# Moving a key norm, four weight scans and two weight loads in the first layer of a linear-attention kernel

## The chip, the cores and the metric

The kernel runs on one core of a Trainium2 chip. The metric is device time in microseconds (us) of one execution of the whole program. Executions of one kernel on one chip mostly agree within some 0.3%. The share of TensorE's full speed that the profile shows for a stretch is called the granted clock; 0.50 is "half clock". Chips differ a little. Kernels are compared only within the same rounds.

## The reference, cut to what matters

Two blocks, each run twice with the same weights: linear attention (A), then a gated bilinear block (B). S is 2048, D 1024, 32 heads of 32, F 3584, all weights in bf16.

```python
def _A_ref(x, wqkv, wo):
    q, k, v = ...                                  # x @ wqkv, in heads
    phi = lambda t: jnp.where(t > 0, t + 1, jnp.exp(t)) + 1e-6
    pq, pk = phi(q), phi(k)
    kv = jnp.einsum("bhsd,bhse->bhde", pk, v)
    z = jnp.einsum("bhsd->bhd", pk)
    num = jnp.einsum("bhqd,bhde->bhqe", pq, kv)
    den = jnp.einsum("bhqd,bhd->bhq", pq, z)[..., None] + 1e-6
    return (num / den)... @ wo

x = A_x
x = x + _A_ref(_layernorm(x), A_wqkv, A_wo)
x = x + _B_ref(_layernorm(x), B_w_gate, B_w_up, B_w_down)   # (g * u) @ w_down
# ... and both once more
```

The kernel works partly in f16, and scales its operands by norms of weights. So it needs, once, a sum of squares of the key weights (the "key norm") and of the three large matrices of block B (the "scans": 42 pieces of 512 KB, each loaded, squared and summed by one ScalarE instruction). All this happens in the first layer, beside its matmuls.

## The kernel before

The stages of the first layer, in TensorE's order: key projection ("k stage"); products of key features with the normalised input, mixed with query tiles ("x and q stage"); values times that ("kv"), query tiles mixed with small products with the output weights ("join"); the output tiles; then block B, the second layer. The parts that the change touches:

```python
def load_o():                                    # output weights, 2 x 1 MB, ScalarE's queue
    for n in range(2):
        nc.scalar.dma_start(out=wo[n], in_=wo_v[:, :, n * NB:(n + 1) * NB])

wv = [head(3), head(1)]                          # value weights live in K[3] and K[1] ...
scan_a = [K[i][:, j * 2 * D:(j + 1) * 2 * D] for i in (3, 1) for j in range(2)]   # ... where early scans do

EARLY, MID, SYNC = 24, 32, 16
scan_buf = [scan_a[i % 4] for i in range(EARLY)] + [scan_c[i % 4] for i in range(NSCAN - EARLY)]

def scan_fetch():                                # loads go out as far ahead as buffers allow
    while scanned[1] < scanned[2]:
        i = scanned[1]
        if any(scan_buf[j] is scan_buf[i] for j in range(scanned[0], i)) or i >= max(EARLY, scanned[0] + 3):
            return
        (nc.sync if i < SYNC else nc.gpsimd).dma_start(out=scan_buf[i], in_=scan_src(i))
        scanned[1] += 1

def scan_step(n=1):
    for _ in range(n):
        i = scanned[0]
        m, c = divmod(i, NU)
        nc.scalar.activation(out=scan_buf[i], in_=scan_buf[i], func=ACT.Square, accum_out=acc[:, m, c:c + 1])
        scanned[0] += 1
        if i in (EARLY - 3, EARLY - 1):          # a buffer is free: value weights, 1 MB each
            n = (i - EARLY + 3) // 2
            nc.scalar.dma_start(out=wv[n], in_=wqkv_v[:, :, 2 * D + n * NB:2 * D + (n + 1) * NB])
        scan_fetch()

# k stage, unit i of the loop (two units are one tile of 128 rows from tile 4 on)
if i == 2:      # sum of squares of each partition's key weights
    nc.vector.tensor_reduce(out=part[:, 3:4], in_=acc[:, 3:4, :], axis=AX.X, op=ALU.add)
elif i == 3:    # 4 bytes a partition to DRAM ...
    nc.sync.dma_start(out=WS[:, :], in_=part[:, 3:4])
elif i == 6:    # ... and back as a row to every partition
    nc.sync.dma_start(out=row, in_=WS[:, :].rearrange("p o -> o p").to_broadcast([P, P]))
elif i == 8:
    nc.vector.tensor_reduce(out=part[:, 3:4], in_=row, axis=AX.X, op=ALU.add)
    ...                                          # maximum, power -1/2
elif i == 9:
    scale_bits(3, 4)
    key_scale()

# end of the x and q stage
x_add(3, 1, QP[b1])
scanned[2] = MID
scan_fetch()
q(7, b0, 2)
scan_step(1)
q(8, a1, 1)
scan_step(1)
q(9, b1, 1)
scan_step(1)
q(10, b0, 2)
load_o()
scan_step(1)
```

## Time and profile before

| | before |
|---|---|
| time, median of 3 runs | 1491.86 us (1490.99 to 1492.01) |
| span of the profiled run | 1488.0 us |
| TensorE without a matmul | 19.0 us |
| k stage ends (first product of the next stage) | 73.92 us |
| kv starts | 164.52 us |
| first output tile starts | 197.60 us |
| first product with TX of block B starts | 256.33 us |

The last four are starts in TensorE's timeline. They cut the run into stretches that each have their own limit. The prediction shows the lines of the waits, of the k stage and of the join. In all such lines, K, ST, TX, XT, MX, W and Q are buffers of the program (Q is the PSUM banks that TensorE writes), and ACTq, SPq or POOL with a DMA is that engine issuing a transfer. Two more rows of the kernel before are needed later, from TensorE's timeline where block B begins (start, duration, then the instruction; a wait would stand in brackets):

```profile
252.88 3.62 PE L1008 MATMUL Q<-XT,K 128*128 128x512 bf16 x16
256.33 1.89 PE L1008 MATMUL Q<-TX,K 128*128 128x512 f16 x8
```

There is no wait between the two rows.

### The profile page before, as it was taken

The numbers are of one execution on the slowest core, as the hardware profiler recorded it, in microseconds if no ns is written. First come the engines' busy times: TensorE is split into PE (matmuls) and PEld (weight loads), VectorE is DVE, ScalarE is ACT, GpSimd is POOL, SyncE is SP. The second block draws the span as 40 slices with busy tenths as digits, with TensorE's granted clock in tenths as the row PEclk, the third lists the DMA queues.
The fourth block names the chain that finished last, engine by engine and source line by source line (L and its number), as shares of the span: only waits on it lengthen the run. The fifth ranks groups of instructions, "written<-read, shape, count | busy, mean of one in ns | idle before, by whom it ended". The sixth has DMA issues, their size and how long they took to land. (4 is left out here: it accounts for less than half of the span.)

```text
span 1488.0 us, 17649 instructions
## 1 busy us (share of the span) xinstructions
PE 1469.0 (99%) x6913; PEld 668.1 (45%) x6913; DVE 1056.5 (71%) x1577; ACT 744.5 (50%) x693; POOL 103.3 (7%) x230
## 2 busy tenths in 40 slices
PE   9899899999999999999999999999999999999999
PEld 3344444444444444444444445444444444444444
DVE  7676788988866477776479778867776845777532
ACT  6678687787700355550087347545563015566200
POOL 2201112000001000000042000200000100000000
PEclk9999999999999999999999999999999999999999
DMA  6466958697647333325739444353332753333442
GB/s 179 119 200 199 282 116 194 199 268 213 214 148 218 82 94 93 88 85 182 221 85 241 71 132 95 64 127 92 86 86 99 243 164 95 85 85 85 154 166 84
DMA packets 267443, 213.29 MB, mean 143 GB/s; under 512 B 102240, under 2 KB 250336, under 8 KB 263776
## 3 DMA queue, kind: packets, MB, share of 16 engines
q1 hardware_dynamic: 254352, 181.63, 43.3%
q0 software_dynamic: 6624, 24.12, 5.8%
q10 hardware_dynamic: 6384, 6.42, 1.3%
q8 instruction: 54, 0.88, 0.3%
q14 instruction: 29, 0.24, 0.1%
HBM read 162.59 MB, written 27.00 MB: 127 GB/s over the span
## 5 line engine op out<-in xcount | busy, mean ns | idle before, releaser
L1008 PEld LDWEIGHTS <-K 128*128 128x128 f16 x3136 | 306.8, 98 | 369.9 <-DVE TX L973 0.2
L1008 PE MATMUL Q<-XT,K 128*128 128x512 bf16 (+1 forms) x1792 | 405.7, 379 | 0.0
L1303 PE MATMUL Q<-K,K 128*128 128x512 f16 (+2 forms) x1582 | 340.4, 377 | 0.0
L1008 PE MATMUL Q<-TX,K 128*128 128x512 f16 x1344 | 308.4, 379 | 0.0
L970 ACT ACTIVATE K<-K,fac 128x2048 f16<-128x2048 bf16 x112 | 224.6, 2008 | 130.5 <-DMA K<-in_B_w_gate_dram 128.4
L1303 PEld LDWEIGHTS <-K 128*128 128x128 f16 x1582 | 154.3, 98 | 184.5
L973 DVE TENSOR_TENSOR K<-K 128x1024 f16<-128x1024 f16 (+1 forms) x244 | 157.3, 666 | 99.1 <-ACT K L970 96.5
L973 DVE TENSOR_TENSOR W<-MX,Q 128x1024 f16<-128x1024 f32 x88 | 107.4, 1220 | 37.4 <-PE Q L1008 18.6
L1028 ACT COPY MX<-Q 128x1024 f32<-128x1024 f32 x60 | 60.8, 1013 | 122.0 <-PE Q L1008 109.6
L973 DVE TENSOR_TENSOR W<-W,Q 128x1024 f16<-128x1024 f32 x80 | 97.6, 1220 | 17.7 <-PE Q L1008 13.2
L1028 ACT COPY W<-Q 128x1024 f32<-128x1024 f32 x52 | 52.6, 1012 | 89.8 <-PE Q L1008 77.3
L419 PE MATMUL Q<-K,K 128*128 128x512 bf16 x384 | 90.5, 391 | 5.1 <-DMA K<-ST 2.2
L973 DVE TENSOR_TENSOR K<-K,K 128x512 f16<-128x512 f16 (+1 forms) x148 | 87.7, 597 | 4.2
L419 PE MATMUL Q<-K,XT 128*128 128x512 bf16 x384 | 86.3, 379 | 1.0 <-DVE rz L464 0.5
L237 ACT ACTIVATE K<-K 128x2048 bf16<-128x2048 bf16 x42 | 79.9, 1907 | 5.4 <-DMA K<-in_B_w_down_dram 3.4
L1012 DVE TENSOR_TENSOR K<-W 128x512 f16<-128x512 f16 x168 | 71.3, 424 | 5.7
L1317 DVE SCALAR_TENSOR_TENSOR W<-Q,kap,X 128x1024 f32<-128x1024 f32 x16 | 20.5, 1284 | 65.7 <-PE Q L1303 65.7
L394 ACT ACTIVATE W<-Q 128x1024 bf16<-128x1024 f32 (+1 forms) x43 | 40.3, 940 | 49.4 <-PE Q L419 49.2
L297 DVE BATCH_NORM_STATS2 st<-X 128x6 f32<-128x512 bf16 x98 | 62.0, 674 | 3.0 <-DMA X<-in_A_x_dram 2.9
L1025 ACT COPY MX<-Q 128x1024 f32<-128x1024 f32 x28 | 28.3, 1009 | 70.2 <-PE Q L1008 57.3
L419 PEld LDWEIGHTS <-K 128*128 128x128 bf16 x384 | 38.0, 100 | 54.4 <-DMA K<-K 5.5
L303 POOL TENSOR_SCALAR ve<-mv 128x1 f32<-128x1 f32 x48 | 12.4, 258 | 704.9 <-DVE mv L301 704.5
(198 smaller groups left out, 1379.5 us busy)
## 6 DMA issues: line engine op xcount, KB each, us to landing
K<-WD SPq DMA_DIRECT2D x28, 1792.0 KB, 7.4
K<-in_B_w_gate_dram SPq DMA_DIRECT2D x70, 512.0 KB, 4.1
K<-in_B_w_up_dram SPq DMA_DIRECT2D x58, 512.0 KB, 5.2
K<-in_A_wqkv_dram SPq DMA_DIRECT2D x8, 1024.0 KB, 6.9
WZ<-K POOLq DMA_DIRECT2D x16, 512.0 KB, 7.0
K<-in_B_w_down_dram POOLq DMA_DIRECT2D x14, 512.0 KB, 6.9
K<-in_B_w_up_dram POOLq DMA_DIRECT2D x12, 512.0 KB, 5.0
K<-in_B_w_down_dram SPq DMA_DIRECT2D x10, 512.0 KB, 5.6
```

Source lines behind the costliest of these rows:

```text
L237: nc.scalar.activation(out=scan_buf[i], in_=scan_buf[i], func=ACT.Square, accum_out=acc[:, m, c:c + 1])
L297: nc.vector.bn_stats(out=stat[t][0][:, c, :], in_=X[:, t, c * NB:(c + 1) * NB])
L394: nc.scalar.activation(out=e, in_=ps, func=ACT.Exp)
L419: nc.tensor.matmul(out=ps, lhsT=xt[:, k, tl * P:(tl + 1) * P], rhs=w[:, k, :], start=(k == 0), stop=(k == KD - 1))
L970: nc.scalar.activation(out=b.bitcast(F16), in_=b, func=ACT.Copy, scale=fac[:, m:m + 1])
L973: eng.tensor_tensor(out=o, in0=a, in1=b, op=op)
L1008: nc.tensor.matmul(out=pair[:, m, :], lhsT=stationary(n, p, m, k), rhs=moving[p][:, k, :], start=(p in (1, 2, 5) and k == 0), stop=(k == K ...
L1012: nc.vector.tensor_tensor(out=hA[i][:, u, :], in0=gu[:, 0, :], in1=gu[:, 1, :], op=ALU.mult)
L1025: nc.scalar.copy(out=snaps[u, 1], in_=a)
L1028: nc.scalar.copy(out=snaps[u, p], in_=a)
L1303: nc.tensor.matmul(out=ps_[:, lo:hi], lhsT=act[:, u, j * P:(j + 1) * P], rhs=w[:, u, lo:hi], start=(p in (1, 2, 5) and u == 0), stop=(u == ...
L1317: stt(out=o, in0=ps_, scalar=kap[:, 0:1], in1=x, op0=ALU.mult, op1=ALU.add)
```

## The change

Its intent: take the round trip through DRAM out of the key norm; use the ScalarE time that this frees for four scans; have the value weights and then the output weights loaded earlier, so that the join doesn't wait for them. Cut to its core:

```diff
-    scan_buf = [scan_a[i % 4] for i in range(EARLY)] + ...
+    scan_buf = [scan_a[i % 4 if i < 18 else 2 + i % 2] for i in range(EARLY)] + ...
-            ... or i >= max(EARLY, scanned[0] + 3):
+            ... or i >= max(EARLY, scanned[0] + 2):
-        for _ in range(n):
+        for _ in range(min(n, scanned[2] - scanned[0])):
-            if i in (EARLY - 3, EARLY - 1):
-                n = (i - EARLY + 3) // 2
+            if i in (18 - 1, EARLY - 1):
+                n = (i + 1) // EARLY
@@ x and q stage
-        q(3, b0, 2)
+        q(3, b0, 3)
@@
-        at_pair(b0)
-        z_column()
@@
         x_add(3, 1, QP[b1])
+        load_o()
+        q(7, b0, 2)
         scanned[2] = MID
         scan_fetch()
-        q(7, b0, 2)
-        scan_step(1)
         q(8, a1, 1)
         scan_step(1)
+        at_pair(a0)
+        z_column()
         q(9, b1, 1)
         scan_step(1)
-        q(10, b0, 2)
-        load_o()
+        q(10, b0, 1)
@@ k stage
-                if 23 <= i <= 29 and i % 2:
+                if 8 <= i <= 11 or i in KSCAN:          # KSCAN = (15, 19, 23, 27)
                     scanned[2] += 1
                     scan_fetch()
+                if i in KSCAN:
+                    scan_step(1)
                 if i == 2:
-                    nc.vector.tensor_reduce(out=part[:, 3:4], in_=acc[:, 3:4, :], ...)
-                elif i == 3:
-                    nc.sync.dma_start(out=WS[:, :], in_=part[:, 3:4])
-                elif i == 6:
-                    nc.sync.dma_start(out=row, in_=WS[:, :]...)
+                    nc.gpsimd.tensor_copy(out=accb[:], in_=acc[:, 3, 0:8])
+                elif i == 5:
+                    norm_ps = mm_tile()
                 elif i == 8:
-                    nc.vector.tensor_reduce(out=part[:, 3:4], in_=row, ...)
-                    nc.vector.tensor_scalar(...)                      # maximum
+                    nc.tensor.matmul(out=norm_ps[:, 0:8], lhsT=ones[:], rhs=accb[:], start=True, stop=True)
+                    nc.scalar.activation(out=acc[:, 3, 0:8], in_=norm_ps[:, 0:8], func=ACT.Copy, accum_out=part[:, 3:4])
+                    nc.gpsimd.tensor_scalar(...)                      # maximum
                     scale_root(3, 4)
-                elif i == 9:
+                elif i == 10:
                     scale_bits(3, 4)
                     key_scale()
@@ join
             if first_A and i > 2:
-                scan_step(1)
+                scan_step(2)
```

A matrix of ones times the 128x8 partial sums puts the sum over partitions into every partition, and ScalarE's accumulator adds the eight columns.

More of the change, by code (lines that the diff above doesn't have):

```diff
@@ L85 @@
     QP = [QQ[:, 2 * i:2 * i + 2, :] for i in range(4)]
-    WS = dram.tile([P, 1], F32, name="WS")
     WZ = [dram.tile([P, D + 64], F32, name=f"WZ{i}")[:, 0:D] for i in range(4)]
@@ L201 @@
     acc = const.tile([P, 4, NU], F32, tag="acc", name="acc")
-    nc.gpsimd.memset(acc[:, 3, :], 0.0)
     fac = const.tile([P, 4], F32, tag="fac", name="fac")
@@ L208 @@
     partb = const.tile([P, 4], BF16, tag="partb", name="partb")
+    accb = const.tile([P, 8], BF16, tag="accb", name="accb")
     SW = 4 * NB
@@ L219 @@
     EARLY, MID, SYNC = 24, 32, 16
-    scan_buf = [scan_a[i % 4] for i in range(EARLY)] + [scan_c[i % 4] for i in range(NSCAN - EARLY)]
+    scan_buf = [scan_a[i % 4 if i < 18 else 2 + i % 2] for i in range(EARLY)] + [scan_c[i % 4] for i in range(NSCAN - EARLY)]
     scanned = [0, 0, 0]
@@ L226, in scan_fetch @@
             i = scanned[1]
-            if any(scan_buf[j] is scan_buf[i] for j in range(scanned[0], i)) or i >= max(EARLY, scanned[0] + 3):
+            if any(scan_buf[j] is scan_buf[i] for j in range(scanned[0], i)) or i >= max(EARLY, scanned[0] + 2):
                 return
@@ L238, in scan_step @@
             scanned[0] += 1
-            if i in (EARLY - 3, EARLY - 1):
-                n = (i - EARLY + 3) // 2
+            if i in (18 - 1, EARLY - 1):
+                n = (i + 1) // EARLY
                 nc.scalar.dma_start(out=wv[n], in_=wqkv_v[:, :, 2 * D + n * NB:2 * D + (n + 1) * NB])
             scan_fetch()
-    row = W[:, 0:2 * P].bitcast(F32)
     def scale_sum(lo, hi):
@@ L1119 @@
     SCALED = 7
+    KSCAN = (15, 19, 23, 27)
     def layer_A(li, R=None):
@@ L1188, in layer_A @@
                 if i == 2:
-                    nc.vector.tensor_reduce(out=part[:, 3:4], in_=acc[:, 3:4, :], axis=AX.X, op=ALU.add)
-                elif i == 3:
-                    nc.sync.dma_start(out=WS[:, :], in_=part[:, 3:4])
-                elif i == 6:
-                    nc.sync.dma_start(out=row, in_=WS[:, :].rearrange("p o -> o p").to_broadcast([P, P]))
+                    nc.gpsimd.tensor_copy(out=accb[:], in_=acc[:, 3, 0:8])
+                elif i == 5:
+                    norm_ps = mm_tile()
                 elif i == 8:
-                    nc.vector.tensor_reduce(out=part[:, 3:4], in_=row, axis=AX.X, op=ALU.add)
-                    nc.vector.tensor_scalar(out=part[:, 3:4], in0=part[:, 3:4], scalar1=2.0 ** -10, scalar2=None, op0=ALU.max)
+                    nc.tensor.matmul(out=norm_ps[:, 0:8], lhsT=ones[:], rhs=accb[:], start=True, stop=True)
+                    nc.scalar.activation(out=acc[:, 3, 0:8], in_=norm_ps[:, 0:8], func=ACT.Copy, accum_out=part[:, 3:4])
+                    nc.gpsimd.tensor_scalar(out=part[:, 3:4], in0=part[:, 3:4], scalar1=2.0 ** -10, scalar2=None, op0=ALU.max)
                     scale_root(3, 4)
-                elif i == 9:
+                elif i == 10:
                     scale_bits(3, 4)
```

## The prediction

> **What bounds the kernel now.** I read the busy table first, then TensorE's waits, then the timeline around each wait. Busy table:
>
> ```profile
> PE 1469.0 (99%) x6913; PEld 668.1 (45%) x6913; DVE 1056.5 (71%) x1577; ACT 744.5 (50%) x693; POOL 103.3 (7%) x230
> ```
>
> TensorE is the bound: 1469.0 of 1488.0 us, so only 19.0 us of the span is without a matmul. The change leaves every large matmul in place. It can only win idle time and the half-speed time that follows it. The waits of TensorE (total, times, longest):
>
> ```profile
> PE Q L932 <- DMA TX<-in_A_wo_dram: 5.3, 1, 5.3
> PE Q L419 <- DMA K<-ST: 2.2, 1, 2.2
> PE Q L419 <- ACT W L408: 1.9, 2, 1.7
> ...
> PE Q L419 <- DMA K<-K: 1.0, 2, 0.5
> ...
> PE Q L932 <- DMA ST<-in_A_wo_dram: 0.6, 1, 0.6
> ...
> PE Q L419 <- DVE rz L464: 0.5, 1, 0.5
> ```
>
> All six lie in the first layer, in two places: the k stage (key projection, 34 to 74 us) and the join of values and output weights (174 to 180 us). The timeline of TensorE in the k stage, start and duration first:
>
> ```profile
> 33.74 4.91 PE L419 MATMUL Q<-K,XT 128*128 128x512 bf16 x22
> 40.85 8.77 PE L419 MATMUL Q<-K,K 128*128 128x512 bf16 x32 [2.20 <-DMA K<-ST]
> 50.14 3.63 PE L419 MATMUL Q<-K,K 128*128 128x512 bf16 x16 [0.52 <-DMA K<-K]
> 54.24 3.63 PE L419 MATMUL Q<-K,K 128*128 128x512 bf16 x16 [0.47 <-DMA K<-K]
> 58.05 7.29 PE L419 MATMUL Q<-K,K 128*128 128x512 bf16 x32 [0.18 <-ACT W L408]
> 67.00 7.08 PE L419 MATMUL Q<-K,K 128*128 128x512 bf16 x32 [1.67 <-ACT W L408]
> ```
>
> The reader should see five gaps, and 32 matmuls that take 8.77 us in one row and 7.08 in another: after the first gap the granted clock is 0.50 from 42 to 44 us. What holds the stage back is the key norm's trip through DRAM: a sum per partition is written out, read back as a row to every partition, and summed by VectorE. Timeline of the DMA queue and VectorE:
>
> ```profile
> 39.65 0.33 SPq L1193 DMA_DIRECT2D W<-WS  x1
> 40.07 1.24 SPq L347 DMA_TRANSPOSE K<-ST  x1
> ...
> 44.29 0.29 DVE L1195 TENSOR_REDUCE part<-W 128x1 f32<-128x128 f32 x1 [4.95 <-DMA W<-WS]
> ```
>
> The write (0.5 KB) was issued at 30.60 us and took 9.0 us to land; the transpose issued behind it at 33.24 took 7.6 us where others took 3.1, and tile 8 waits for it. The next transpose stands behind the row's read, which waits for the write. VectorE, in order, sits idle 4.95 us, and the statistics of tiles 11 to 15 slip with it. The second place:
>
> ```profile
> 164.73 0.38 ACTq L161 DMA_DIRECT2D ST<-in_A_wo_dram  x1
> 165.14 0.59 ACTq L161 DMA_DIRECT2D TX<-in_A_wo_dram  x1
> ...
> 179.70 0.61 PE L932 MATMUL Q<-TX,W 128*128 128x512 bf16 x1 [5.30 <-DMA TX<-in_A_wo_dram]
> 180.10 3.62 PE L419 MATMUL Q<-K,K 128*128 128x512 bf16 x8
> ```
>
> The output weights are asked for at 165 us and land after 9.3 and 14.5 us; afterwards 8 matmuls take 3.62 us, where they take 1.89 later.
>
> **What the Trainium skill says.** "TensorE: Matmul & The Clock Gate", section "What's actually happening": an idle window of about 3.4 us brings the clock to half, and about 3.4 us of work brings it back; the window runs freely. The trace agrees on the half (0.50 at 42 to 44 and at 180 to 184 us), but a gap of only 2.20 us was enough once, while 1.67 us was not. "DMA: Bandwidth & Descriptors", section "Specifications": under 512 B a transfer is a read-modify-write; section "Issuing engines are not separate DMA queues": all queues share the same 16 engines. The 4 bytes per partition that took 9.0 us fit this, though no view shows the read-modify-write itself. The second statement means that moved scan loads can delay transposes. "VectorE: DVE Perf Modes", section "Why `tensor_reduce` can't reduce along partition axis": there is no path between lanes, hence the old round trip; a product with ones is another way to sum partitions.
>
> **The change part by part.** First I price what could be won, by matmul counts at the steady 0.2157 us from start to start (16 take 3.45).
>
> (a) K stage. 22 matmuls from 33.74 end their issue at 38.49. The 8 remaining tiles need 8 x 16 x 0.2157 = 27.6 us, so the stage could end at 66.1. The next stage starts at 73.92. Lost: 7.8 us (5.0 of listed gaps, 1.7 of half clock as 8.77 - 7.08, the rest pipeline drain at each gap). The change removes the write, the read, two reductions on VectorE and the maximum there. It adds on GpSimd a copy of 128x8 and a maximum (about 0.25 us each, as the 258 ns row of L303), one 128x8 matmul, and on ScalarE a 128x8 copy with a sum (estimated 0.3 with its accumulator read of 0.19). VectorE goes on at 39.34 instead of 44.29, and its next statistics start at about 39.4 instead of 46.6. The scale bits, 1.2 us, follow later.
>
> What is added to this stage: four scans on ScalarE, each about 1.9 us (the x42 row's 1907 ns), so 7.6 us; and six scan loads of 512 KB (four of them early) between the transposes. I walked the engines by hand with the durations above. Tile 10's transpose lands near 44.6 us, needed at 45.5. Tile 11's stands behind two scan loads (1 MB, 2.7 us at the 380 GB/s seen at 41 to 43) and lands near 49.5, needed at 49.0. Tile 14's: statistics 53.5, ScalarE done 56.5, landing about 60, needed at 59.4. ScalarE falls some 5 us behind, so the pairs of banks come free just in time, and the first combination of the next stage, whose copies stand behind two more scans, costs about 1 us. Loss left: 2 us. **Win 5.8 us.**
>
> (b) Output weights, issued now before q tile 7, about 14 us earlier. From 173.27 (24 matmuls after 168.09) to the first output tile stand 72 matmuls, 15.5 us: 188.8. Before, it started at 197.60. Lost: 8.8 us (5.3 + 0.6 of waits, some 2.6 of half clock). With 14 us more lead, 14.5 us of landing is hidden. ScalarE then needs 3.93 us for each q tile with its two copies (starts 1.01, 1.01, 0.91, 1.0 apart) against TensorE's 4.31, so it keeps up. **Win 8.8 us.**
>
> (c) The reciprocal of z moves from before q 5 to after q 8: its 0.62 us between matmul groups goes. **Win 0.6 us.**
>
> (d) Value weights in two steps and scans on two buffers. Scans 18 to 23 alternate two buffers, so a scan waits about 5 us for its load; I find ScalarE about 4 us late for q tile 4 and 3 us for q tile 5, always caught up before TensorE needs a bank. **Zero.**
>
> (e) Output stage. The order of instructions on GpSimd shows a loss: before, five scan loads stood ahead of the power for the weight scales, now four. That power waited until 209.21 us. So ScalarE now has its fifth scan behind the load that follows it, and the first weight conversion behind that scan:
>
> ```profile
> 210.47 2.00 ACT L970 ACTIVATE K<-K,fac 128x2048 f16<-128x2048 bf16 x1 [2.08 <-DVE fac L266]
> 215.92 1.91 ACT L237 ACTIVATE K<-K 128x2048 bf16<-128x2048 bf16 x1 [3.44 <-DMA K<-in_B_w_down_dram]
> ```
>
> The conversion used the 3.44 us of waiting; now it comes after, and all behind it is 1.9 + 2.0 = 3.9 us later relative to TensorE. The norms of the next layer stand at its end; the last transposes landed at 252.65, and the product that needs them started with 0.2 us of weight wait, so there is no slack but some 1 us of room in the transpose queue. **Loss 3 us.**
>
> Sum: 5.8 + 8.8 + 0.6 - 3.0 = 12.2 us. Time: 1491.86 - 12.2 = 1479.7 us.
>
> **The rivals.** First, all is hidden: (e) costs nothing and the k stage runs dry; the win is 7.8 + 8.8 + 0.6 = 17.2, time 1474.7. For it speaks that ScalarE has slack over the stages (50% busy); against it, tile 14's narrow margin. Second, the k stage changes its bound: scans and their loads make ScalarE or the transposes the new wait, the gaps stay and one is long enough for half clock: (a) wins 1 to 2, time about 1484. For it speaks 7.6 us of added work on an engine that feeds VectorE; against, ScalarE's old idle 3.48 us before L324 at 62.61. Third, (e) grows past 3 us and the clock halves at the start of the second layer: a loss of 5 or 6, time about 1482. A loss overall would need 17 us of new waits; nothing shows so many.
>
> **Range and chances.** From all hidden (1474.7) to the second and third together (1486 or 1487): 1474.5 to 1486. A gain over 2% needs 1462, 30 us, more than all idle and half-clock time. Faster 0.01, same 0.98, slower 0.01.
>
> **What would show it.** Right: no wait on output weights and a clock of 1.00 there; no DRAM row; the k stage ends at 67 to 69 us; first output tile near 183 to 185 instead of 197.60; then a new wait of about 3 us at the first products of the second layer, with ScalarE's scan waiting for its load in the output stage. Wrong: half clock still in the k stage, the new wait absent, or TensorE waiting on banks in the query stage.

## The result, and the profile after

| | before | after |
|---|---|---|
| time, median (range) | 1491.93 us (1490.99 to 1494.48) | 1477.83 us (1477.17 to 1480.55) |
| ratio, 95% interval | | .9906 [.9889, .9924] |
| span of the profiled run | 1488.0 | 1475.4 |
| k stage ends | 73.92 | 68.35 |
| kv starts | 164.52 | 158.91 |
| first output tile starts | 197.60 | 183.20 |
| first TX product of block B starts | 256.33 | 243.54 |

A ratio is the mean time of one kernel's fast runs over that of the other's of the same rounds, so not quite the ratio of the medians. The change wins 14.1 us in the medians and 12.6 in the two profiled spans; 12.2 were predicted, and a gain of under 2% was forecast with a chance of 0.98. The rest of this text asks whether it came as predicted.

The busy table after:

```profile
PE 1460.0 (99%) x6822; PEld 667.7 (45%) x6914; DVE 1055.7 (72%) x1574; ACT 744.5 (50%) x695; POOL 103.3 (7%) x231
```

No engine has noticeably less to do; the win is time in which TensorE waited or ran at half clock. (The two PE times can't be subtracted: half clock counts as busy, and some 90 matmul records are missing here, 6822 beside 6914 weight loads.) TensorE's waits after (total, times, longest):

```profile
PE Q L416 <- DMA K<-K: 1.5, 2, 1.1
PE Q L1004 <- DVE TX L969: 1.3, 1, 1.3
...
PE Q L416 <- ACT acc L1193: 0.5, 1, 0.5
```

The waits for output weights, for the transposes K<-ST and for ScalarE's W in the k stage are gone. Three smaller ones are new or larger. TensorE's timeline in the k stage after:

```profile
31.27 0.17 PE L1192 MATMUL Q<-accb,ones 128*128 128x8 bf16 x1
31.30 5.34 PE L416 MATMUL Q<-K,XT 128*128 128x512 bf16 x23
37.16 1.89 PE L416 MATMUL Q<-K,XT 128*128 128x512 bf16 x8 [0.52 <-ACT acc L1193]
38.89 10.52 PE L416 MATMUL Q<-K,K 128*128 128x512 bf16 x47
50.52 10.53 PE L416 MATMUL Q<-K,K 128*128 128x512 bf16 x47 [1.11 <-DMA K<-K]
61.44 7.08 PE L416 MATMUL Q<-K,K 128*128 128x512 bf16 x31 [0.39 <-DMA K<-K]
```

The whole norm is now a product of 0.17 us, and the granted clock is 1.00 throughout. The gap of 0.52 comes from a shared bank: the norm's product took a PSUM bank that the next tile needs, and ScalarE empties it late. The gap of 1.11 is tile 11's transpose behind two scan loads. At the join and at the start of block B, same view:

```profile
167.66 0.38 PE L928 MATMUL Q<-ST,W 128*128 128x512 bf16 x1
167.88 0.38 PE L928 MATMUL Q<-TX,W 128*128 128x512 bf16 x1
168.09 1.89 PE L416 MATMUL Q<-K,K 128*128 128x512 bf16 x8
...
183.20 3.62 PE L938 MATMUL Q<-K,XT 128*128 128x512 bf16 x15
...
238.58 3.62 PE L1004 MATMUL Q<-XT,K 128*128 128x512 bf16 x16
243.54 1.90 PE L1004 MATMUL Q<-TX,K 128*128 128x512 f16 x8 [1.34 <-DVE TX L969]
```

The join has no gap left; block B has the predicted new one, of 1.34 us.

Differences of the starts give each stretch's share: k stage 73.92 - 68.35 = 5.6 won; from there to kv 90.60 against 90.56, nothing; from kv to the first output tile 33.08 against 24.29, 8.8 won; from there to block B's TX products 58.73 against 60.34, 1.6 lost; the rest of the run 0.2 lost. Sum 12.6.

The loss, seen from ScalarE after the change, in its timeline of the output stage:

```profile
200.39 1.91 ACT L236 ACTIVATE K<-K 128x2048 bf16<-128x2048 bf16 x1 [6.40 <-DMA K<-in_B_w_down_dram]
202.30 1.99 ACT L966 ACTIVATE K<-K,fac 128x2048 f16<-128x2048 bf16 x1
```

A scan waits 6.40 us for its load, and the first weight conversion now stands behind it. Before, the conversion was ahead and used that waiting time.

### The profile page after: what moved, and what is told of

The parts are those of the page before. It is cut to its first block, busy times and chain, and to the rows that moved or that the text cites. A ratio compares the mean times of both kernels' runs of the same rounds, so it can differ in the third digit from the quotient of the medians.

```text
span 1475.4 us, 17550 instructions
## 1 busy us (share of the span) xinstructions
PE 1460.0 (99%) x6822; PEld 667.7 (45%) x6914; DVE 1055.7 (72%) x1574; ACT 744.5 (50%) x695; POOL 103.3 (7%) x231
## 5 line engine op out<-in xcount | busy, mean ns | idle before, releaser
L1004 PE MATMUL Q<-XT,K 128*128 128x512 bf16 (+1 forms) x1734 | 396.4, 379 | 3.1
L416 PE MATMUL Q<-K,K 128*128 128x512 bf16 x375 | 86.0, 379 | 2.0 <-DMA K<-K 1.5
```

The lines of the kernel that those rows point to most:

```text
L416: nc.tensor.matmul(out=ps, lhsT=xt[:, k, tl * P:(tl + 1) * P], rhs=w[:, k, :], start=(k == 0), stop=(k == KD - 1))
L1004: nc.tensor.matmul(out=pair[:, m, :], lhsT=stationary(n, p, m, k), rhs=moving[p][:, k, :], start=(p in (1, 2, 5) and k == 0), stop=(k == K ...
```

## The experiments

Twelve runs follow, all with correct results; each is compared with the kernel before. Early output weights, key norm alone, both together and three loads ahead share one chip.

**Early output weights alone.** Is the 8.8 us at the join bought by the move of the load alone?

```diff
         x_add(3, 1, QP[b1])
+        load_o()
         scanned[2] = MID
@@
         q(10, b0, 2)
-        load_o()
```

> The kernel before with only the output weights asked for earlier (before q tile 7 instead of after q tile 10). Theory (part b by itself): the waits of 5.3 and 0.6 us and the half clock after them go, 8.8 us less, time about 1483.1; the k stage keeps its five gaps and ends near 74 us; no new wait at the start of the second layer. Rival (the two parts share their gain, because ScalarE or VectorE is late in the join once the weights are there): 5 us or less, time over 1486, and a new wait of TensorE between 172 and 190 us.

Measured: 1486.90 us (1485.86 to 1488.36) against 1491.75, ratio .9964 [.9946, .9983]: 4.9 us won, not 8.8. ScalarE's timeline, then TensorE's:

```profile
152.67 5.59 ACTq L161 DMA_DIRECT2D TX<-in_A_wo_dram  x1
158.37 1.02 ACT L394 ACTIVATE W<-Q 128x1024 bf16<-128x1024 f32 x1 [6.81 <-issue]
```
```profile
171.87 5.34 PE L419 MATMUL Q<-K,K 128*128 128x512 bf16 x24 [2.42 <-ACT W L398]
178.84 0.39 PE L932 MATMUL Q<-ST,W 128*128 128x512 bf16 x1 [1.64 <-DVE W L924]
```

The weights themselves were in time. In the profiled run the stretch from kv to the first output tile took 29.05 us, 4.0 less than the old 33.08, and the k stage ended 1.2 us later than in the old profile, at 75.12. But the second half of the value weights had gone out at 151.59 and the first half of the output weights at 152.00, and the issue of the third 1 MB load held ScalarE's queue for 5.59 us. ScalarE was late for the query tiles, the transposes of those tiles landed after 12.8 us (median), VectorE waited 3.5 us for one of them, and TensorE waited for ScalarE and for VectorE. So the load's early place isn't enough.

**Later by one query tile.** The same load moved only to the place after query tile 7, to see whether the blocked issue was the whole of it (this one ran on a second chip, like the first tiny write, the wide write and the first attempt below).

```diff
         q(7, b0, 2)
+        load_o()
         scan_step(1)
@@
         q(10, b0, 2)
-        load_o()
```

> The kernel before with the output weights asked for one q tile later than in o_early (after q 7, before q 8). In o_early the second output-weight load held ScalarE 5.59 us at its issue, 1 us behind the second value-weight load, and TensorE later waited 2.4 us on ScalarE and 1.8 us on VectorE. Theory (it is the third 1 MB load issued within 1.1 us on ScalarE's queue that spoils the gain): with 3.4 us between, the issue takes 1 us or less, those waits go, and the part is worth about 8 us, time about 1483.5. Rival (the loads and the transposes contend for the DMA engines however they are issued): TensorE still waits 2 us or more between 165 and 182 us, and no more than 6 us are won.

Measured: 1488.33 us against 1489.35, ratio .9995 [.9975, 1.0015]: nothing won in the time. In the trace the stretch from kv to the first output tile is 2.4 us shorter (30.66), but the one after it is 1.3 longer (60.03). The theory wanted an issue of 1 us or less; it took 2.14 us, although the third load now went out 4.4 us after the first (154.79 - 150.41). So the block was milder; yet the transposes of the query tiles landed after 15.3 us and the two halves of the weights after 11.1 and 23.3. VectorE waited 5.29 us, until 173.73, for one of those transposes (XT<-MX), and TensorE's main wait at the join is for VectorE:

```profile
PE Q L932 <- DVE W L924: 3.5, 1, 3.5
```

So a blocked issue isn't the whole of it: here VectorE, and TensorE behind it, waited for a late transpose. The DMA engines were busy without a break from 152 to 166 us, so that the loads delayed it is likely; no run takes the loads away.

**Key norm alone.**

```diff
 (all k-stage lines of the key norm as in the change; scans, value weights, output weights and z as before)
```

> The kernel before with only the key norm summed by TensorE and ScalarE (no DRAM trip; scans, weights as before). Theory (the DRAM trip is what held the k stage): the transpose of tile 8 lands in about 3 us instead of 7.6, no half clock, the k stage ends near 67.5 us (before 73.9), time about 1485.5. Rival (the k stage is held by VectorE's statistics in any case, the trip only covers it): the gap moves to a later tile, the stage ends at 71 us or later, less than 3 us won.

Measured: 1486.91 us (1486.06 to 1487.98), ratio .9965 [.9944, .9987]. The k stage ended at 68.89, 5.0 us sooner, with one larger gap left there (1.61 us, ScalarE's W) and no half clock. So the key norm alone pays nearly all of the k stage's win, as the first theory had it. At the join, however, TensorE's waits grew from 5.9 to 7.1 us:

```profile
PE Q L930 <- DMA TX<-in_A_wo_dram: 4.4, 1, 4.4
PE Q L930 <- DMA ST<-in_A_wo_dram: 2.7, 1, 2.7
```

The total win of 4.8 missed the expectation by about that much: part of what one stage wins ahead of a load that isn't early enough is waited off again.

**Key norm and early output weights, without the scans' part.** Both at once, with scans, value weights and z as before.

```diff
 (key norm as in the change)
         x_add(3, 1, QP[b1])
+        load_o()
@@
         q(10, b0, 2)
-        load_o()
```

> The kernel before with the key norm and the early output weights, but the scans, the value weights and the reciprocal of z as before. Theory (the scan part wins nothing and costs 1.5 us in the output stage): 1491.9 - 6.4 - 8.8 = 1476.7, so equal to the changed kernel or up to 2 us faster; no wait of TensorE for TX at the first products of the second layer. Rival (the scans had to move to make room on ScalarE for the rest): 2 us or more slower than the changed kernel, with TensorE waiting on ScalarE in the query stage.

Measured: 1481.57 us (1481.08 to 1483.40), ratio .9930 [.9912, .9949], 3.7 us above the changed kernel's median of its own call. This decides what the remaining parts are worth. ScalarE's timeline and TensorE's:

```profile
147.00 5.72 ACTq L160 DMA_DIRECT2D TX<-in_A_wo_dram  x1
```
```profile
166.33 7.03 PE L417 MATMUL Q<-K,K 128*128 128x512 bf16 x24 [2.56 <-ACT W L396]
```

The same block as in the first experiment, a gap of 2.56 us, and half clock after it (24 matmuls in 7.03 us instead of 5.34). From kv (160.03) to the first output tile (189.43) are 29.40 us; the changed kernel needs 24.29. So 5.1 of the 8.8 us at the join depend on the parts that this kernel leaves out: the scans' new places and buffers (one scan fewer between query tiles 7 and 8, and four scan loads issued after tile 7), the value weights in two steps, z, and the number of postponed VectorE steps after query tiles 3 and 10. The price of those parts is the loss in the output stage, which this kernel hasn't got (58.73 us from output tile to block B, as before).

**Scan loads three ahead, as before.** The changed kernel with one number put back.

```diff
-            ... or i >= max(EARLY, scanned[0] + 2):
+            ... or i >= max(EARLY, scanned[0] + 3):
```

> The changed kernel with the scan loads issued up to three ahead again (5 instead of 4 of them stand before the power of the weight scales on GpSimd). Theory (part e of the prediction: the missing fifth load delays ScalarE's chain in the output stage): ScalarE's scan no longer waits 6.4 us there, the 1.3 us wait of TensorE for TX at the start of the second layer goes, time about 1.5 us below the changed kernel. Rival (the second layer waits for VectorE or the transpose queue all the same): the wait of 1.3 us stays.

Measured: 1476.57 us (1476.08 to 1478.94), ratio .9898 [.9878, .9917]. TensorE's wait at block B is gone, and ScalarE's first conversion is at 199.19 us with only 0.29 us of waiting ahead of it, although this run's first output tile started 3.0 us later than the changed kernel's. So the order of five or four loads ahead of the power on GpSimd was the cause of the loss, as the prediction had it. From the first output tile to block B are 58.82 us again (58.73 before the change, 60.34 after it), and so they are in the two attempts below that also keep three loads ahead (58.82, 58.83). The time is 1.3 us lower, less than the runs spread (the profiled run was the slowest of its four, 1478.94); the traces carry this, not the time.

**A tiny write put back.** What was slow in the old round trip? A write of 4 bytes a partition, in the place of the old one, added to the changed kernel.

```diff
+    WS = dram.tile([P, 1], F32, name="WS")
@@ if i == 2: ... 
+                elif i == 3:
+                    nc.sync.dma_start(out=WS[:, :], in_=acc[:, 3, 0:1])
```

> The changed kernel with a DRAM write of 4 bytes per partition (128 partitions) put back into the sync queue where the old one stood; nobody reads it[...]. Theory (the tiny write itself holds the transposes behind it): it takes about 9 us to land, tile 8's transpose takes over 6 us instead of 3.0, TensorE waits 1.5 us or more before tile 8, and the time rises by 2 to 5 us. Rival (only the read-back and the wait in the queue held them): the transpose still lands in about 3 us and the time stays within 1 us.

Measured: 1480.95 us in its one run; the write landed after 9.9 us and the transposes K<-ST after 7.8. But TensorE's main wait was 4.0 us for ScalarE's acc: that instruction rewrites the buffer that my write was reading, so it had to wait for the write. That is a fault of the experiment, and its time says nothing. It was mended later, with a constant as the source:

```diff
+                elif i == 3:
+                    nc.sync.dma_start(out=WS[:, :], in_=one6[:])
```

> After, plus a write of four bytes a partition to HBM, now from a constant that nothing rewrites, while the tile of the fourth step is in work; so, unlike in the first try, ScalarE has nothing of its own to wait for. Theory (the small pieces themselves hold the transposes): the write takes 9 to 10 us, the transposes of tile 8 land in over 6 us (3.0 in after), TensorE waits 2 to 4 us for them and the time is 2 to 5 us above after's. Rival (only the buffer that was rewritten did it): the write may be slow, but the wait before tile 8 stays under 0.3 us and the time within 1 us of after's.

Measured: 1478.29 us in one run (the changed kernel: 1477.43 to 1481.67). TensorE's timeline:

```profile
38.03 1.89 PE L417 MATMUL Q<-K,XT 128*128 128x512 bf16 x8 [0.83 <-ACT acc L1196]
40.74 3.63 PE L417 MATMUL Q<-K,K 128*128 128x512 bf16 x16 [0.82 <-DMA K<-ST]
45.57 0.60 PE L417 MATMUL Q<-K,K 128*128 128x512 bf16 x2 [1.20 <-DMA K<-ST]
```

The two waits for K<-ST are back, 2.0 us in all, and the k stage ends at 69.75, 1.4 us later than after the change. The time doesn't show it: so small a loss is inside the runs' spread. The mechanism holds, its size in the time was expected too large. And the write by itself brings back 1.4 us of the 5.0 us that the key norm alone won in the k stage; the rest goes with the read-back, VectorE's wait for it and the half clock, which no run takes apart. Its counterpart with wide pieces, 1024 bytes a partition:

```diff
+    WS = dram.tile([P, 512], BF16, name="WS")
+                elif i == 3:
+                    nc.sync.dma_start(out=WS[:, :], in_=X[:, 0, 0:NB])
```

> As tiny_write, but 1024 bytes per partition (128 KB) instead of 4. If the smallness of the pieces is what makes it slow, this write of 256 times the bytes lands in 4 us or less and tile 8's transpose in under 5 us, with no wait of TensorE there; if any write to DRAM at this place is slow, it looks as in tiny_write.

Measured: 1477.10 us in one run, no wait for K<-ST. The issues of both kernels from 15 to 45 us (size, median us from issue to landing), first with the tiny write from the constant, then with the wide write:

```profile
K<-ST SPq DMA_TRANSPOSE x2, 7.2
WS<-one SPq DMA_DIRECT2D x1, 0.5 KB, 9.3
```
```profile
WS<-X SPq DMA_DIRECT2D x1, 128.0 KB, 2.0
...
K<-ST SPq DMA_TRANSPOSE x2, 3.6
```

256 times as many bytes took less than a quarter of the time and held up nothing. Not the write as such, but 128 pieces of 4 bytes are slow, and transposes issued behind them are slow with them, in these single runs.

**A first attempt at a better version.** The changed kernel with three loads ahead, the norm's product two units sooner, and the early scan fetches three units later.

```diff
-                if 8 <= i <= 11 or i in KSCAN:
+                if 11 <= i <= 14 or i in KSCAN:
-                elif i == 8:      # norm product
+                elif i == 6:
-                elif i == 10:     # scale bits
+                elif i == 8:
     (and scanned[0] + 3)
```

> The changed kernel with three mends: scan loads three ahead (as ahead3), the norm's product and copy after tile 4 instead of tile 5 (the changed kernel's TensorE waits 0.5 us on that copy before the second half of tile 7, which uses the same bank), and the four early scan loads behind the transposes of tiles 11 and 12 instead of between 9 and 12 (tile 11's transpose took 7.3 us and TensorE waited 1.1 us). Theory: all three waits go, with their drains some 3.5 us less than the changed kernel, about 1474.3. Rival: the k stage is then held by ScalarE or VectorE and only the 1.5 us of ahead3 are won.

Measured: 1477.54 us against 1489.35, ratio .9926 [.9907, .9944]. The waits at the shared bank and at block B were gone, but two transposes now stood behind the moved loads (waits of 1.42 and 1.47 us), and the k stage ended at 69.53. The moved fetch gave it back.

The last four share a third chip (the mended tiny write above is one of them).

**The value weights' second half back, just ahead of the output weights.** Does the join's win hang on the order of these loads?

```diff
-            if i in (18 - 1, EARLY - 1):
+            if i == 18 - 1:
@@
         x_add(3, 1, QP[b1])
+        nc.scalar.dma_start(out=wv[1], in_=wqkv_v[:, :, 2 * D + NB:2 * D + 2 * NB])
         load_o()
```

> After with one thing moved back: the second half of the value weights is not issued after the 24th scan, some 8 us ahead of the output weights, but directly before them, so three loads of 1 MB are issued in a row. Theory (the output weights pay only because the value weights are out of the way): the second output load's issue holds ScalarE 5 us or more, TensorE waits 2 to 5 us at the join for tiles that ScalarE and VectorE bring late, and the time is 3 to 5 us above after's (about 1481 to 1483). Rival (order of the loads is free, as the prediction's zero for that part has it): within 1 us of after's and no wait over 0.7 us at the join.

Measured: 1479.30 us (1477.71, 1489.11, 1477.56, 1480.89), ratio .9950 [.9920, .9981]; the changed kernel 1479.42. In the profiled run (1477.71) TensorE has no wait over 0.2 us at the join, and kv to the first output tile take 24.29 us, exactly as after the change. The theory falls for this run, the rival is right. ScalarE's issues in it:

```profile
141.74 0.39 ACTq L844 DMA_DIRECT2D K<-in_A_wqkv_dram  x1
...
144.11 0.37 ACTq L160 DMA_DIRECT2D ST<-in_A_wo_dram  x1
144.52 1.16 ACTq L160 DMA_DIRECT2D TX<-in_A_wo_dram  x1
```

The third load goes out 2.8 us after the first of the three and its issue takes 1.16 us. In the two kernels that were blocked it went out 1.1 us after the first (147.00 - 145.91; 152.67 - 151.59) and took 5.72 and 5.59; after the change it goes out 8.2 us later (144.42 - 136.27) and takes 0.60. In these four traces a larger distance goes with a shorter issue. But the distance isn't shown to be the cause: one query tile later, above, it was 4.4 us, more than here, and the issue took 2.14 us and TensorE waited. Two other things tell good from bad at least as well. GpSimd issued its next four scan loads (2 MB) 0.5 to 4.1 us ahead of the output weights in the three kernels that lost time at the join, and after them in the changed kernel and here. GpSimd with key norm and early load (where the output weights went out at 146.33 and 147.00), then here:

```profile
145.82 2.13 POOL L228 DMA_DIRECT2D K<-in_B_w_up_dram  x4 [11.59 <-PE Q L724]
```
```profile
144.59 2.13 POOL L228 DMA_DIRECT2D K<-in_B_w_up_dram  x4 [14.08 <-PE Q L723]
```

And those three kernels have one scan more on ScalarE between query tiles 7 and 8. Slow landing alone doesn't decide either: here the output weights landed after 12.9 and 18.3 us and the transposes XT<-MX after 12.0 (median), little better than with the early load alone (13.4, 19.5 and 12.8), and TensorE didn't wait. No run separates these. Here the last early scan was done at 137.5, so nothing tied the value weights' load to the output weights' any more; before, that scan ended at 145.7 in the kernel with norm and early load alone, and its buffer is the one that the load needs. The distance may be thin: one run of this kernel took 1489.11 and its clock was .999, but it wasn't profiled, so whether the block came back in it is open.

**A second attempt at a better version, and the changed kernel beside it.** Three loads ahead, norm two units (one tile, not the two of the expectation) sooner, fetches where the change has them.

```diff
-            ... scanned[0] + 2):
+            ... scanned[0] + 3):
-                elif i == 8:      # norm product
+                elif i == 6:
-                elif i == 10:     # scale bits
+                elif i == 8:
```

> After with scan loads three ahead instead of two at the join (the wait of the second layer's first products goes, 1.3 us) and the key norm's product two tiles sooner (the wait for ScalarE at the shared bank, 0.5 us, goes), the scan fetches of the k stage where after has them. Theory: 1.3 to 2.0 us below after in the same call, with neither wait in the profile and the k stage ending at about 67.9. Rival (the gain is given back by transposes behind loads, as in the last try): within 0.7 us of after.

> After itself, unchanged, for a comparison on the same chip: 1477 to 1479 us and .989 to .993 of before's time.

Measured: 1476.35 us (1475.33 to 1477.71), ratio .9910 [.9896, .9923], and for the changed kernel 1479.42 (1477.43 to 1481.67), .9930 [.9917, .9942], both against 1489.47. The new version is 3 us lower in the mean, though the two intervals overlap a little. TensorE's timeline of the new version:

```profile
238.27 3.62 PE L1004 MATMUL Q<-XT,K 128*128 128x512 bf16 x16
241.72 1.89 PE L1004 MATMUL Q<-TX,K 128*128 128x512 f16 x8
```

Neither of the two waits is left. The k stage ends at 68.05, block B's TX products start 1.8 us sooner than after the change, and the span is 1473.6, 1.8 below 1475.4. That is the theory's 1.3 to 2.0; the rest of the 3 us is probably spread of the changed kernel, and its second profile shows where some of it comes from. ScalarE, the same scan in the first profile of the changed kernel and in the second:

```profile
131.77 1.91 ACT L236 ACTIVATE K<-K 128x2048 bf16<-128x2048 bf16 x1 [1.25 <-DMA K<-in_B_w_up_dram]
```
```profile
134.14 1.91 ACT L236 ACTIVATE K<-K 128x2048 bf16<-128x2048 bf16 x1 [3.51 <-DMA K<-in_B_w_up_dram]
```

GpSimd issued the load at 126.94 in one and at 127.03 in the other. In the second it landed about 2.3 us later; TensorE then waited for VectorE in two more places (0.8 and 1.0 us) and the span was 1477.6, 2.2 more. Scans that alternate between two buffers have no second load in hand, so one late load reaches the matmuls. The run with three loads ahead that was profiled (span 1477.2) shows the same.

## Why the prediction was right, and where it wasn't

- **What bounds it.** Right: TensorE is 99% busy in both with the same large matmuls, and only waits and half clock were won. One reading was wrong: of the six waits listed, the last (0.5 us on rz) lies in neither of the two places but at 136.90 us, in the x and q stage; it is the one that (c) prices.
- **(a) k stage, 5.8.** Right in size (5.6) and cause: the key norm alone won 5.0 (of which the 4-byte write by itself accounts for 1.4). The predicted end of 67 to 69 us was met (68.35). Two terms of the residual were mis-sized: tile 11 waited 1.11 us instead of about 0.5, as its transpose took 7.3 us behind two scan loads; and the 0.52 us at the bank shared with the norm's product was not foreseen. In return the 1 us feared at the next stage didn't come.
- **(b) output weights, 8.8.** The size is exact (8.8), but the reason given, 14 us more lead, is not sufficient. With that lead alone 4.9 us were won in the time (4.0 at the join of its trace), and one query tile later nothing (2.4 at the join, 1.3 of them lost after it).
- **(c) z's reciprocal, 0.6.** The old wait went, but the stretch from k stage to kv didn't get shorter (90.60 and 90.56 us): new waits of 0.2 and 0.3 us took most of it. This step gave nothing here; in the two tiny-write traces the stretch is 90.0, so some 0.6 us seem to be there when no other wait takes them.
- **(d) value weights and two-buffer scans, "Zero."** This is the step that failed. The words that ScalarE is "always caught up before TensorE needs a bank" hold for the profiled run, but the part isn't worth zero: without it and z's move, 5.1 of (b)'s 8.8 us are not there. In the three kernels that had the early load without it, ScalarE or VectorE was late for the query tiles, and TensorE waited 2.4 to 3.5 us for them. The sum came out right because (b) was priced as if (d) were present, so the two were priced together without being seen together. It has a cost too: from the k stage to kv the five traces with the old scan buffers take 90.6 us each, the nine with the new ones 90.0 to 93.6. Which piece of (d) does it stays open. The place of the value weights' second half isn't needed, in the run that was traced; the scan left out before query tile 8, the order against GpSimd's scan loads, the buffers, the postponed VectorE steps and z were not separated.
- **(e) output stage, loss 3.** Mechanism right, size wrong: 1.6. Predicted was a chain 3.9 us later; it was 2.7 (the next layer's norms began at 223.12, and at 234.86 before, which is 220.46 on the changed kernel's scale). The scan's load had landed 4.8 us after its issue, 6.0 before, so the scan could start sooner than reckoned. TensorE's gap was 1.34.
- **The rivals.** None took place as a whole. The second was right that transposes behind scan loads become a wait, wrong that the k stage would keep its gaps. What no rival foresaw is what decided (b): that an early load alone can make ScalarE and the transposes late, so that TensorE waits for them in place of the weights.

The single terms together: predicted 5.8 + 8.8 + 0.6 + 0 - 3 = 12.2; in the traces 5.6 + 8.8 + 0 - 1.6 - 0.2 = 12.6. The error of 1.4 in (e) was nearly cancelled by 0.6 in (c) and 0.4 elsewhere; that the total is so close is luck to that extent. And one error of reasoning didn't show in the sum at all.

## What to carry to other kernels

A load moved forward need not win its full wait: here it won 4.0 of the 8.8 us at the join by itself, and the rest only with the other parts of the change. Look at the issue times of its neighbours, on all queues, at how long each issue holds the engine and at what that engine must do next, and price the parts of a change together where one clears the way for another. A sum over partitions by a small product with ones beat the trip through DRAM here, 5.0 us in the k stage, in part because transposes stood behind the tiny write. When a sum agrees with the measurement, check its terms in the traces, for errors of reasoning can hide in a right total.

## What the Trainium skill lacked or had wrong

- "DMA: Bandwidth & Descriptors", section "Specifications", says that transfers under 512 B are a read-modify-write. Neither that row nor the page's section on small descriptors says how long such a transfer takes to land or what it costs others: 128 pieces of 4 B took 9.0 to 9.9 us, and transposes behind them 6.4 to 7.8 us (median) instead of 3.6, while 128 pieces of 1024 B landed in 2.0 us and held up nothing. The read-modify-write itself shows in no view.
- The same page, section "Issuing engines are not separate DMA queues", says that the time to initiate a DMA is "usually small relative to the DMA itself". The third of three 1 MB loads issued within 1.1 us held ScalarE for 5.59 and 5.72 us (it landed after 19.5 and 19.1), and TensorE then waited 2.42 and 2.56 us for ScalarE. What made the issue so long isn't settled here.
- "TensorE: Matmul & The Clock Gate", section "What's actually happening", gives an idle window of about 3.4 us for the fall to half clock, and says that it runs freely. Here the clock halved after gaps of 2.20 and 2.56 us and not after 2.42 and 1.67. So gaps well under 3.4 us weren't safe, and gaps of nearly the same length weren't always punished.
- "VectorE: DVE Perf Modes", section "Why `tensor_reduce` can't reduce along partition axis", sends such a reduction to GpSimd. It doesn't mention a product with ones. Here that cost TensorE 0.17 us, and ScalarE 0.17 and 0.20 for the copy and the accumulator read; the cost to look for is the bank it takes (0.52 us of waiting in the changed kernel, none when the product stood two units sooner).
